# Attention values of three units made together, with three buffers for transposed exponentials and two for decoded words

## The chip, the cores and the metric

The program runs on one core of a Trainium2 chip. The metric is the device time of one execution in microseconds (us). Five engines work side by side, each with its own queue of instructions: TensorE (PE, matrix multiplies; PEld is its weight load), VectorE (DVE), ScalarE (ACT), GpSimd (POOL) and SyncE (SP, which here only issues DMA transfers). They wait for each other on semaphores.

## What is computed

Attention with a local window and a few global columns, then two chains of dense layers, all in float32:

```python
scores = q @ k.T / 8 + bias          # 4 batches, 8 heads, 768 positions, 64 wide
a = softmax(scores where key is one of 8 global or of the last 96 positions)
x = a @ v                            # -> 3072 tokens x 512
x = ((x @ w1) * (x @ w2)) @ w3 @ w_out
h = x @ w_in                         # 512 -> 2048
out = (h * cos(h)) @ w_out2          # 2048 -> 512
```

## The kernel before

**Units and slots.** Attention is cut into 96 units: one unit is 128 query positions of one pair of heads. Twelve units (four head pairs, p, times three position tiles, i) make one block of 384 tokens, and there are eight blocks. After a lead of 14 units, which are made beside the product w3 @ w_out, the main loop runs in slots. Slot n holds the scores of unit n, its maximum, exponential and normalisation, the transposes of unit n - 1, the values of unit n - 2 (the product of the transposed exponentials with v), and one step of the dense layers of an earlier block: in the first eight slots of a block two groups of twelve matmuls of the "up" layers, in the last four two groups of twelve of the "down" layer. The whole order is written out by hand, one queue per engine.

**One slot on each engine.** PE: four score matmuls (lines 544 and 548, into `s_ps`), the values (line 628, into `x_ps`), twelve dense matmuls (lines 391 to 393, into `mm`), the transposes (601, 603, into `pt_ps`), twelve more dense matmuls. DVE: the product of the dense halves (671), the maximum (564), decoding steps, the low half of a dense product (678), the copy of finished values (643), the low half of a coming unit's keys (519, 522), the reciprocal (588), more decoding steps. ACT: the high half of a coming unit (512), of a dense product (675), a decoded word tile (329, 331), the exponential (575), the finished values (642), the dense copy (667), the copy of the transposes to SBUF (611, tile `pt`), another word tile. POOL scales the exponentials (592).

**Values.** `a_values(n)` takes the two tiles `pt` (copied from PSUM in slot n + 1) and `v` (loaded by DMA, line 505) and writes 128 columns of `x_ps`, a PSUM tile of 384 columns which three units of one head pair share; after the third, `a_out` copies it out (642, 643). A matmul of the values fills 64 of PE's columns (form 128*64 or 104*64 in the profile), one per head; every other matmul of the stage fills 128. A unit has 8 matmul records in the trace, or 4 where it lies at the start of a sequence. `pt` and `e` have two buffers, `v` and `qk` three.

**Decoding.** The weights come as 64-bit words. For each of 72 tiles ACT makes `x` and `s` (329, 331), DVE shifts (335), sets signs (339) and adds (347). The last 32 tiles (w_in and w_out2) are then stored to HBM (line 351, `late_w<-x`) for later use. The buffers of `x` are a ring: `x` can be written again only when the store of the tile that had the buffer before has landed. In the first eight slots of the main loop six decoding steps are made in each slot (three steps to a tile), later three in two slots.

**Numbering.** Unit 14 starts at 104 us in the trace, unit 23 at 173 us, and the last values are made at 602 us.

Of the kernel before, what the change touches and what calls it, by code (L numbers as in the profile page):

```python
# [8 lines left out]
F32 = mybir.dt.float32  # L9
# [20 lines left out]
TPB = TB // 128  # L30
# [6 lines left out]
LEAD = 14  # L37
# [225 lines left out]
def fused(ctx, tc, a_qk, a_v, w3p, wo1p, w1p, w2p, winp, wo2p, n_global, n_local, out):  # L263
    nc = tc.nc

    def pool(name, bufs, side="left", space=None):
        kw = {} if space is None else {"space": space}
        if space is None:
            kw["side"] = side
        return tc.alloc_tile_pool(name=name, bufs=bufs, reuse_waits="tile", **kw)  # L270
# [9 lines left out]
    misc = pool("misc", 1)  # L280
    wts = pool("wts", 8)
    attn = pool("attn", 2)
# [19 lines left out]
    rings, taken = {}, {}  # L302
# [50 lines left out]
    def late_load(name, pair):  # L353
        t = raws[name, pair] = misc.tile([128, 2, 512], F32, tag="raw", name="raw", bufs=3)
        src = late_w[0 if name == "in" else 1, 2 * pair:2 * pair + 2]
        nc.sync.dma_start(out=t, in_=src.rearrange("a p b -> p a b"))
# [122 lines left out]
    def where(n):  # L479
        j, r = divmod(n, UPB)  # L480
        p, i = divmod(r, TPB)
        return j, p, i, (TPB * j + i) % (S // 128)

    plain = {}
    qk_raw, v_raw, hh, kl, es, sts, pts, xps, xT = {}, {}, {}, {}, {}, {}, {}, {}, {}

    def a_load(n):
        if not LEAD <= n < NU:
            return
        t = attn.tile([128, QK_W], F32, tag="qk", name="qk", bufs=3)  # L490
        nc.sync.dma_start(out=t, in_=a_qk[n])
        qk_raw[n] = t
# [8 lines left out]
    def a_load_v(n):  # L501
        if not 0 <= n < NU:
            return
        t = attn.tile([128, 2, 128], F32, tag="v", name="v", bufs=3)
        nc.sync.dma_start(out=t.rearrange("p a b -> p (a b)"), in_=a_v[n])
        v_raw[n] = t

    def a_split_hi(n):
        if not LEAD <= n < NU:
            return  # L510
        hh[n] = attn.tile([128, QK_W], F32R, tag="hh", name="hh")
        nc.scalar.copy(out=hh[n], in_=qk_raw[n])  # L512
# [16 lines left out]
    def a_scores(n):  # L529
        if not 0 <= n < NU:  # L530
            return
        s_ps[n] = p_s.tile([128, 2, WIN], F32, tag="s", name="s_ps")
        if n in plain:
            t = plain.pop(n)
            for e in range(2):
                nc.tensor.matmul(
                    s_ps[n][:, e, :], lhsT=t[:, e * 128:(e + 1) * 128],
                    rhs=t[:, 256 + e * WIN:256 + (e + 1) * WIN], start=True, stop=True,
                )
            return  # L540
        t, l = hh.pop(n), kl.pop(n)
        for e in range(2):
            q = t[:, e * 128:(e + 1) * 128]
            nc.tensor.matmul(
                s_ps[n][:, e, :], lhsT=q, rhs=t[:, 256 + e * WIN:256 + (e + 1) * WIN],
                start=True, stop=False,
            )
            nc.tensor.matmul(  # L548
                s_ps[n][:, e, :], lhsT=q, rhs=l[:, e * WIN:(e + 1) * WIN],
                start=False, stop=True,  # L550
            )
# [53 lines left out]
    def a_tcopy(n):  # L605
        if not 0 <= n < NU:
            return
        t = where(n)[3]
        pts[n] = attn.tile([128, 2, 2, 128], F32, tag="pt", name="pt")
        if t:  # L610
            nc.scalar.copy(  # L611
                out=pts[n].rearrange("p a b c -> p (a b c)"),
                in_=pt_ps.rearrange("p a b c -> p (a b c)"),
            )
        else:
            nc.scalar.copy(out=pts[n][:, :, 0, :], in_=pt_ps[:, :, 0, :])

    def a_values(n):
        if not 0 <= n < NU:
            return  # L620
        j, p, i, t = where(n)
        if i == 0:
            xps[j, p] = p_x.tile([128, TB], F32, tag="x", name="x_ps")
        x, pt, vt = xps[j, p], pts.pop(n), v_raw.pop(n)
        for c in range(2 if t else 1):
            kk = NPV if c else 128
            for e in range(2):
                nc.tensor.matmul(  # L628
                    x[e * 64:(e + 1) * 64, i * 128:(i + 1) * 128],
                    lhsT=vt[:kk, c, e * 64:(e + 1) * 64], rhs=pt[:kk, e, c, :],  # L630
                    start=c == 0, stop=c == (1 if t else 0),
                )
# [36 lines left out]
    def up_mult(j, m):  # L669
        ab_f[m] = moe.tile([128, TB], F32, tag="ab_f", name="ab_f", bufs=1)  # L670
        nc.vector.tensor_tensor(out=ab_f[m], in0=mm_ps.pop("b"), in1=a_sb.pop(m), op=ALU.mult)  # L671

    def up_hi(j, m):
        ab[m] = moe.tile([128, 2, TB], F32R, tag="ab", name="ab", bufs=M1)
        nc.scalar.copy(out=ab[m][:, 0, :], in_=ab_f[m])  # L675
# [21 lines left out]
    def down_out(j, m):  # L697
        ps = mm_ps.pop("d")
        t = x2t[j, m] = moe.tile([128, 2, TB], F32R, tag="x2t", name="x2t", bufs=1)
        nc.scalar.copy(out=t[:, 0, :], in_=ps)  # L700
        nc.vector.tensor_tensor(
            out=t[:, 1, :], in0=ps, in1=t[:, 0, :].bitcast(F32), op=ALU.subtract
        )
# [35 lines left out]
    with tc.manual_schedule():  # L739
# [8 lines left out]
        for o in "3A3A3A3A3A3A3A3ABBBBBBBB":  # L748
# [3 lines left out]
            else:  # L752
                n, m = ups.pop(0)
# [7 lines left out]
        tp = pool("tp", 1, side="right")  # L761
        EARLY = 30
        for i, (key, _, _) in enumerate(dec):
            rings[key] = {"raw": [(misc, 3)], "x": [(attn, 3)], "s": [(attn, 2)]}
            if i < EARLY:
                rings[key]["raw"].append((early, 2))
                rings[key]["x"].append((early, 4))
                rings[key]["s"].append((early, 2))
# [51 lines left out]
        def decode(n):  # L820
            for _ in range(n):
                next(steps_left, None)
# [13 lines left out]
        for c, (h, k) in enumerate(chunks):  # L836
            n = c - 2
# [47 lines left out]
        def late(i):  # L885
            if i % 2 == 0:
                return "in", i // 2 + 2
            return ("in", 7) if i == 3 else ("o2", (i - 5) // 2)
# [4 lines left out]
        def x2_load(J, p, tag):  # L893
            t = x2in[J] = p.tile([128, MO, 2, TB2], F32R, tag=tag, name=tag, bufs=1)
            for m in range(MO):
                nc.gpsimd.dma_start(out=t[:, m], in_=x2s[m, :, :, J * TB2:(J + 1) * TB2])

        for j in range(NB1):
            for i in range(UPB):
                sl = j * UPB + i  # L900
                n = sl + LEAD
                last = j == NB1 - 1
                if last and i == 0:
                    attn.release()
                    w2p_ = pool("w2p", 6)
                a_load(n + 4)
                a_load_v(n + 1)
                if last:
                    if i < 3:
                        late_load("in", i)  # L910
                    elif i == 10:
                        late_load("o2", 3)
                    if 2 <= i < 10:
                        late_load(*late(i))
                    if i == 4:
                        x2_load(0, w2p_, "x2in")
                a_scores(n)
                a_values(n - 2)
                a_split_hi(n + 2)
                if 1 <= i <= M1:  # L920
                    up_mult(j, i - 1)
                    up_hi(j, i - 1)
                a_max(n)
                decode(3 if sl < 8 else sl % 2)
                if i == 0 and j > 0:
                    down_out(j - 1, MO - 1)
                    down_store(j - 1, MO - 1)
                elif i > M1:
                    down_out(j, i - M1 - 1)
                    down_store(j, i - M1 - 1)  # L930
                if 1 <= i <= M1:
                    up_lo(j, i - 1)
                a_exp(n)
                a_out(n - 2)
                a_split_lo(n + 2)
                if i < M1:
                    up(j, i, "a")
                    up_copy(j, i)
                else:
                    down(j, i - M1, 0)  # L940
                a_transpose(n - 1)
                a_tcopy(n - 1)
                a_norm(n)
                decode(3 if sl < 8 else 1)
                if i < M1:
                    up(j, i, "b")
                else:
                    down(j, i - M1, 1)
                if last:
                    if i < 3:  # L950
                        run(late_split("in", i, "wC", w2p_))
                    if 2 <= i < 10:
                        run(late_split(*late(i), "wB" if i % 2 else "wA"))
# [75 lines left out]
        for s in range(len(steps) + LAG):  # L1029
# [14 lines left out]
            if s < len(steps):  # L1044
                if J == 0 and m < 5:
                    tag = ("Wa", "Wa", "Wb", "Wb", "wD")[m]
# [85 lines left out]
```

## Time and profile before

| | |
|---|---|
| median of 3 runs | 1190.04 us (1188.34 to 1190.36) |
| the profiled execution | 1191.22 us, its span 1189.4 us |
| lead, 0 to 104.4 us | PE busy 86.9 us |
| main loop, first nine slots, 104.4 to 173.4 | PE busy 57.4 of 69.0 us, DVE 63.1 |
| main loop, the rest, 173.4 to 602.0 | PE busy 428.6 of 428.6 us, DVE 252.1 |
| second chain, 602.0 to 1189.4 | PE busy 578.2 of 587.4 us |

A busy PE is not PE at its peak: matmuls are pipelined and their ends are modelled, so what a step costs is read from the starts of the matmuls that follow each other. The span runs from the first to the last instruction; the time of an execution is some 2 us longer.

### The profile page before, as it was taken

What the parts mean: (1) busy time and instruction counts of PE and PEld (TensorE: products, weight loads), DVE (VectorE), ACT (ScalarE), POOL (GpSimd) and SP (SyncE); (2) the same over time, 40 slices, a digit from 0 to 9 for tenths busy, and PEclk for the clock granted to TensorE, in tenths of its full rate; (3) what the DMA queues carried; (4) which work ended last, traced back from release to release, by engine and by line L of the source; (5) the groups of instructions that cost most, each with busy time, mean ns of one, the idle gap of its engine ahead of it and who ended that gap; (6) DMA issues with size and microseconds to landing.
All of it is one profiled execution on the core that took longest, in us unless ns stands there. A gap on an engine that the chain in (4) does not pass through costs nothing. (4 is left out here: it accounts for less than half of the span.)

```text
span 1189.4 us, 17345 instructions
## 1 busy us (share of the span) xinstructions
PE 1151.1 (97%) x6178; PEld 985.5 (83%) x6178; DVE 769.1 (65%) x1756; ACT 579.6 (49%) x1256; POOL 124.9 (10%) x213
## 2 busy tenths in 40 slices
PE   4998899999999999999999999999999999999997
PEld 1445789999999999999999888888888888888885
DVE  7899986766676555545424666666666666665664
ACT  5777775656566555555434533333333333333332
POOL 0000221111111111111114200000000000000000
PEclk9999999999999999999999999999999999999999
DMA  8776685555554434333145311102102002000001
GB/s 260 251 227 223 232 284 197 176 191 167 168 190 146 132 96 138 90 113 110 45 159 191 125 45 48 59 1 70 38 1 71 36 1 72 36 1 21 16 1 38
DMA packets 65295, 132.72 MB, mean 112 GB/s; under 512 B 6576, under 2 KB 27184, under 8 KB 65200
## 3 DMA queue, kind: packets, MB, share of 16 engines
q1 hardware_dynamic: 58672, 118.95, 30.9%
q0 software_dynamic: 6528, 12.58, 3.7%
q8 instruction: 50, 0.82, 0.3%
q14 instruction: 45, 0.37, 0.1%
HBM read 104.25 MB, written 27.26 MB: 111 GB/s over the span
## 5 line engine op out<-in xcount | busy, mean ns | idle before, releaser
L592 POOL TENSOR_SCALAR e<-e,st 128x232 f32<-128x232 f32 (+1 forms) x164 | 84.5, 528 | 507.3 <-DVE st L588 173.5
L991 ACT ACTIVATE r<-r 128x512 f32<-128x512 f32 x96 | 60.7, 632 | 153.7 <-DVE r L987 153.7
L1000 ACT CAST g<-r 128x512 fp32r<-128x512 f32 x96 | 59.6, 621 | 139.5 <-DVE r L996 139.5
L512 ACT CAST hh<-qk 128x720 fp32r<-128x720 f32 x82 | 65.1, 794 | 118.6 <-PE s_ps L548 111.5
L993 DVE SCALAR_TENSOR_TENSOR r<-r 128x512 f32<-128x512 f32 x96 | 66.5, 693 | 70.0 <-ACT r L991 69.9
L1001 DVE TENSOR_TENSOR g<-r,g 128x512 fp32r<-128x512 f32 x96 | 66.5, 693 | 66.0 <-ACT g L1000 66.0
L575 ACT ACTIVATE e<-e,top 128x232 f32<-128x232 f32 (+1 forms) x192 | 89.3, 467 | 6.9 <-DVE top L564 6.8
L564 DVE CUSTOM_DVE_ANT_0 e<-s_ps,bias 128x232 f32<-128x232 f32 (+1 forms) x192 | 65.5, 378 | 41.8 <-PE s_ps L548 38.8
L391 PE MATMUL mm<-ab,W 128*128 128x384 f32 x256 | 91.8, 358 | 0.5 <-ACT ab L675 0.5
L391 PE MATMUL mm<-xT,wA 128*128 128x384 f32 x256 | 91.7, 358 | 0.0
L391 PE MATMUL mm<-xT,wB 128*128 128x384 f32 x256 | 91.1, 356 | 0.0
L393 PE MATMUL mm<-xT,wA 128*128 128x384 f32 x256 | 86.9, 339 | 0.0
L393 PE MATMUL mm<-ab,W 128*128 128x384 f32 x256 | 86.6, 338 | 0.0
L392 PE MATMUL mm<-xT,wA 128*128 128x384 f32 x256 | 86.4, 338 | 0.0
L392 PE MATMUL mm<-ab,W 128*128 128x384 f32 x256 | 86.3, 337 | 0.1
L393 PE MATMUL mm<-xT,wB 128*128 128x384 f32 x256 | 86.1, 336 | 0.0
L392 PE MATMUL mm<-xT,wB 128*128 128x384 f32 x256 | 85.7, 335 | 0.0
L984 DVE SCALAR_TENSOR_TENSOR r<-kt,h_ps 128x512 f32<-128x512 int32 x96 | 65.7, 684 | 24.3 <-ACT kt L982 24.3
L671 DVE TENSOR_TENSOR ab_f<-mm,a_sb 128x384 f32<-128x384 f32 x64 | 35.5, 555 | 67.5 <-PE mm L393 67.5
L842 PE MATMUL mm<-wo,w 128*128 128x512 f32 x128 | 64.9, 637 | 12.7 <-DVE wo L347 12.7
L982 ACT ACTIVATE kt<-h_ps 128x512 int32<-128x512 f32 x96 | 57.3, 597 | 29.3 <-PE h_ps L393 29.2
L628 PE MATMUL x_ps<-pt,v 128*64 128x128 f32 (+1 forms) x704 | 59.8, 286 | 11.6 <-ACT pt L611 11.4
(189 smaller groups left out, 3017.9 us busy)
## 6 DMA issues: line engine op xcount, KB each, us to landing
qk<-in_a_qk SPq DMA_DIRECT2D x82, 360.0 KB, 3.2
v<-in_a_v SPq DMA_DIRECT2D x97, 128.0 KB, 2.1
x2s<-x2t SPq DMA_DIRECT2D x32, 384.0 KB, 2.9
raw<-in_w3p SPq DMA_DIRECT2D x16, 512.0 KB, 4.7
raw<-in_winp SPq DMA_DIRECT2D x16, 512.0 KB, 4.0
late_w<-x SPq DMA_DIRECT2D x32, 256.0 KB, 2.2
raw<-in_wo2p SPq DMA_DIRECT2D x16, 512.0 KB, 4.1
raw<-late_w SPq DMA_DIRECT2D x16, 512.0 KB, 4.5
```

The costliest lines, as they stand in the source:

```text
L391: nc.tensor.matmul(ps, lhsT=l_hi, rhs=r_hi, start=first and i == 0, stop=False)
L392: nc.tensor.matmul(ps, lhsT=l_hi, rhs=r_lo, start=False, stop=False)
L393: nc.tensor.matmul(ps, lhsT=l_lo, rhs=r_hi, start=False, stop=last and i == n - 1)
L512: nc.scalar.copy(out=hh[n], in_=qk_raw[n])
L564: nc.vector.tensor_tensor_reduce(out=es[n][:, e, :w], in0=sp[:, e, :w], in1=bias[:, 2 * p + e, :], scale=-0.125, scalar=3.0e38, op0=ALU.ad ...
L575: nc.scalar.activation(es[n][:, e, :w], es[n][:, e, :w], ACTF.Exp, bias=top[:, n, e:e + 1], scale=-1.0, accum_out=sts[n][:, 0, e:e + 1],)
L592: (engine or nc.gpsimd).tensor_scalar(es[n][:, e, :w], es[n][:, e, :w], st[:, 1, e:e + 1], 1.0, ALU.mult, ALU.mult)
L842: nc.tensor.matmul(W_ps[m], lhsT=wt["w3", c][:, m * 128:(m + 1) * 128], rhs=wt["wo1", k], start=k == 0, stop=k == M1 - 1,)
L984: nc.vector.scalar_tensor_tensor(out=r, in0=kt, scalar=-C1, in1=ps, op0=ALU.mult, op1=ALU.add)
L991: nc.scalar.activation(r, r, ACTF.Sin, scale=0.5)
L993: nc.vector.scalar_tensor_tensor(out=r, in0=r, scalar=-2.0, in1=r, op0=ALU.mult, op1=ALU.mult)
L1001: nc.vector.tensor_tensor(out=t[:, 1, :], in0=r, in1=t[:, 0, :].bitcast(F32), op=ALU.subtract)
```

## The change

`a_values` is no longer called in every slot for unit n - 2. In every third slot, where n - 2 is the third unit of a head pair, it is called for units n - 4, n - 3 and n - 2, one after the other. So that the transposed exponentials of three units can wait, `pt` gets three buffers (TPB is 3). The ring of decoded words `x` has two buffers in place of three for all tiles from the thirty-first on (six in place of seven for those before). The load of `v` moves: slot n loads unit n - 1, behind the values, where it had loaded unit n + 1 ahead of them; the first main slot loads none and the second loads unit 14 a second time (one load more in all). The number of matmuls is unchanged.

```diff
-        pts[n] = attn.tile([128, 2, 2, 128], F32, tag="pt", name="pt")
+        pts[n] = attn.tile([128, 2, 2, 128], F32, tag="pt", name="pt", bufs=TPB)
...
-            rings[key] = {"raw": [(misc, 3)], "x": [(attn, 3)], "s": [(attn, 2)]}
+            rings[key] = {"raw": [(misc, 3)], "x": [(attn, 2)], "s": [(attn, 2)]}
...
-                a_load_v(n + 1)
...
                 a_scores(n)
-                a_values(n - 2)
+                if (n - 2) % TPB == TPB - 1:
+                    for u in range(n - 1 - TPB, n - 1):
+                        a_values(u)
+                if n > LEAD:
+                    a_load_v(n - 1)
```

On PE, at the scores of unit 45 before (the numbers in the names are buffers; mm and xT belong to the dense layers; x4 are four matmuls of the program, eight records in the trace):

```order
L393 MATMUL mm_3338<-xT_2795,wB_1078 128x384
L544 MATMUL s_ps_3355<-hh_3216 128x232
L548 MATMUL s_ps_3355<-kl_3234,hh_3216 128x232
L544 MATMUL s_ps_3355<-hh_3216 128x232
L548 MATMUL s_ps_3355<-kl_3234,hh_3216 128x232
L628 MATMUL x_ps_3291<-pt_3331,v_3137 64x128 x4
L391 MATMUL mm_3382<-xT_2161,wB_1126 128x384
```

On PE now, at the scores of unit 46, the next third slot:

```order
L393 MATMUL mm_3403<-xT_2793,wB_1158 128x384
L544 MATMUL s_ps_3418<-hh_3289 128x232
L548 MATMUL s_ps_3418<-kl_3302,hh_3289 128x232
L544 MATMUL s_ps_3418<-hh_3289 128x232
L548 MATMUL s_ps_3418<-kl_3302,hh_3289 128x232
L628 MATMUL x_ps_3423<-pt_3254,v_3212 64x128 x4
L628 MATMUL x_ps_3423<-pt_3324,v_3287 64x128 x4
L628 MATMUL x_ps_3423<-pt_3390,v_3351 64x128 x4
L391 MATMUL mm_3457<-ab_2917,W_537 128x384
```

Three units stand in a row between the scores and the dense matmuls; in the two slots between, the dense matmuls follow the scores at once.

On ACT nothing moves, but the waits differ. Before, in the slot of unit 18, where two word tiles are made (the words in brackets are the semaphores, DMAHW those of transfers; of the two DMAHW of line 329, one is the tile's own load and one the store of the tile three earlier):

```order
L329 ACTIVATE x_1304<-raw_1211 128x512 [waits DMAHW6_49,DMAHW5_49]
L331 ACTIVATE s_1306<-raw_1211 128x512 [waits Activation_49]
L575 ACTIVATE e_1295,st_1296<-e_1295,top_85 128x232 [waits DVE_49] x2
L667 COPY a_sb_1328<-mm_1315 128x384 [waits PE_49,Activation_49]
L611 COPY pt_1334<-pt_ps_88 128x512 [waits PE_49]
L329 ACTIVATE x_1345<-raw_1255 128x512 [waits DMAHW7_49,DMAHW0_49]
```

The same place now:

```order
L329 ACTIVATE x_1297<-raw_1209 128x512 [waits DMAHW6_49,DMAHW5_49]
L331 ACTIVATE s_1299<-raw_1209 128x512 [waits Activation_49]
L575 ACTIVATE e_1288,st_1289<-e_1288,top_85 128x232 [waits DVE_49] x2
L667 COPY a_sb_1321<-mm_1308 128x384 [waits PE_49,Activation_49]
L611 COPY pt_1327<-pt_ps_88 128x512 [waits PE_49]
L329 ACTIVATE x_1338<-raw_1253 128x512 [waits DMAHW7_49,DMAHW2_49,DVE_49]
```

The order is the same; the second transfer that line 329 waits for is now the store of the tile two earlier.

## Rows read from the trace of the kernel before

**Rows 1.** Busy time by stretch: PE, PEld, DVE, ACT, POOL, clock, DMA share, GB/s.

```profile
104.40:173.40 69.00, 57.44 (x362) 52.99 (x361) 63.09 (x158) 52.78 (x121) 15.26 (x17) 0.95 0.73 246
173.40:602.00 428.60, 428.60 (x2893) 403.62 (x2892) 252.08 (x784) 244.34 (x622) 69.24 (x148) 1.00 0.44 139
602.00:1189.40 587.40, 578.21 (x2620) 486.18 (x2618) 363.03 (x541) 209.16 (x356) 39.11 (x40) 1.00 0.16 51
```

**Rows 2.** PE's waits, whole span: total us, times, longest.

```profile
PE x_ps L628 <- ACT pt L611: 11.4, 7, 2.5
```

**Rows 3.** Timeline of PE, one slot with 8 value records: start, duration.

```profile
300.57 0.27 PE L544 MATMUL s_ps<-hh 128*128 128x232 f32 x1
...
300.91 0.27 PE L548 MATMUL s_ps<-kl,hh 128*128 128x232 f32 x1
301.11 0.66 PE L628 MATMUL x_ps<-pt,v 128*64 128x128 f32 x8
301.70 0.44 PE L391 MATMUL mm<-xT,wB 128*128 128x384 f32 x1
301.98 0.34 PE L392 MATMUL mm<-xT,wB 128*128 128x384 f32 x1
...
303.73 0.34 PE L393 MATMUL mm<-xT,wB 128*128 128x384 f32 x1
```

**Rows 4.** Timeline of PE, a slot with 4 value records.

```profile
191.09 0.27 PE L548 MATMUL s_ps<-kl,hh 128*128 128x232 f32 x1
191.30 0.44 PE L628 MATMUL x_ps<-pt,v 128*64 128x128 f32 x4
...
191.95 0.34 PE L392 MATMUL mm<-xT,wA 128*128 128x384 f32 x1
```

**Rows 5.** Timeline of PE, from the transposes to the dense matmuls, same slot.

```profile
304.12 0.27 PE L601 MATMUL pt_ps<-ident,e 128*128 128x128 f32 x1
304.23 0.27 PE L603 MATMUL pt_ps<-ident,e 128*104 128x128 f32 x1
304.26 0.42 PE L391 MATMUL mm<-xT,wB 128*128 128x384 f32 x1
304.52 0.33 PE L392 MATMUL mm<-xT,wB 128*128 128x384 f32 x1
```

**Rows 6.** Busy time in that slot, columns as in rows 1.

```profile
300.57:306.45 5.88, 5.88 (x42) 5.55 (x42) 4.01 (x12) 4.26 (x10) 0.90 (x2) 1.00 0.58 165
```

**Rows 7.** Busy time in the decoding slots, columns as in rows 1.

```profile
129.00:168.00 39.00, 32.19 (x218) 29.38 (x217) 36.78 (x92) 30.98 (x72) 10.61 (x12) 1.00 0.82 287
```

**Rows 8.** SP's queue, stores of decoded words: issue time.

```profile
129.51 0.33 SPq L351 DMA_DIRECT2D late_w<-x  x1
...
136.83 0.33 SPq L351 DMA_DIRECT2D late_w<-x  x1
...
157.33 0.33 SPq L351 DMA_DIRECT2D late_w<-x  x1
```

**Rows 9.** Landing of stores: the eleven from 129 to 165 us; those of 136.83 and 157.33.

```profile
DMA to landing us min/median/max: 2.0/3.0/4.8
...
DMA to landing us min/median/max: 4.6/4.6/4.6
...
DMA to landing us min/median/max: 4.8/4.8/4.8
```

**Rows 10.** Timeline of ACT and DVE: a word tile made, and three shifts.

```profile
138.11 0.69 ACT L329 ACTIVATE x<-raw 128x512 f32<-128x512 f32 x1
...
133.85 0.41 DVE L335 TENSOR_SCALAR x<-x 128x512 int32<-128x512 int32 x1
...
140.38 0.41 DVE L335 TENSOR_SCALAR x<-x 128x512 int32<-128x512 int32 x1
...
160.87 0.41 DVE L335 TENSOR_SCALAR x<-x 128x512 int32<-128x512 int32 x1
```

**Rows 11.** The word tiles of line 329 from 173 us on: durations, first and last start.

```profile
L329 ACT ACTIVATE x<-raw x19: 666/671/689, 177.9 to 385.4; 128x512 f32<-128x512 f32 x19
```

## The prediction

> **What bounds the kernel now.** I read the busy time by stretch first [rows 1]. From 173.4 to 602.0 us PE is busy for the whole 428.6 us, with DVE at 252.1 and ACT at 244.3: there the order and the pace of PE's matmuls set the time. In the nine slots before that, 104.4 to 173.4 us, PE is busy for 57.4 of 69.0 us, and PE's waits name the reason: 11.4 us in seven waits of the values for `pt`, ACT's copy of the transposes [rows 2]. That copy is late because DVE is: from 129 to 168 us DVE is busy for 36.8 of 39.0 us and ACT for 31.0 [rows 7], and the small rest is mostly the gaps between DVE's instructions. So the change meets two regimes. Behind 173.4 us it is worth what PE saves; ahead of it, it is worth what DVE saves or loses. The second chain, from 602.0 us on, isn't touched.
>
> **What a visit to the values costs PE.** The timeline of one slot shows it [rows 3]. Three score steps take 300.91 - 300.57 = 0.34 us, or 0.113 each. The last score starts at 300.91; the second dense matmul behind the values starts at 301.98, 1.07 us later. Without values between them this would be one score step and one dense step. A dense step is (303.73 - 301.98) / 10 = 0.175 us (ten steps to the twelfth matmul). So the visit costs 1.07 - 0.113 - 0.175 = 0.78 us. In a slot with four value records in place of eight the same stretch is 191.95 - 191.09 = 0.86 us [rows 4], and the visit costs 0.57. Four records more thus cost 0.21 us, eight cost 0.42, and 0.78 - 0.42 = 0.36 us of the visit don't depend on the number of records. It lies at the edges: 0.20 us from the last score to the first value where a step is 0.113, 0.59 us from there to the first dense matmul where the eight records account for 0.42, and 0.28 us for that dense matmul where a step is 0.175. I use 0.35 us (the rows are rounded to 0.01).
>
> Whether that is an edge of every change of kind, the transposes tell: from their last one at 304.23 to the second dense matmul at 304.52 are 0.29 us, and a transpose step (0.11) with a dense step (0.175) makes 0.285 [rows 5]. Going from transposes back to dense matmuls costs nothing; they fill 128 columns as the dense ones do, the values fill 64. So the cost belongs to going over to the 64-column form and back, and three units in a row pay it once.
>
> **The sum behind 173.4 us.** Slots 23 to 97 make the values of 75 units, 75 visits before and 25 now. 50 visits less at 0.35 us are **17.5 us**. All of it lies on the path, since PE never idles there. The values themselves (0.42 us or 0.21 us a unit) only move: two slots shrink from 5.88 to about 5.1 us, the third grows to about 6.75; together 16.9 in place of 17.6 us. What has to keep up with a slot of 5.1 us is DVE with 4.0 us of work and ACT with 4.3 [rows 6], in slots that a longer one always follows. I cost that at nothing; the cover is about 0.8 us a short slot, and a miss would be paid back in the long one.
>
> The third `pt` buffer and the later `v` load are free here. A load of `v` now stands one slot or more ahead of its use, and only in each third slot does SP wait for the values at that place, as it did in every slot before; the loads of `qk`, the stores and the word loads queued behind it on SP wait no longer than they did. The one load more is not on the path.
>
> **The ring of decoded words.** Here is the price. From the thirty-first tile on `x` has two buffers, so ACT can write a tile only when the store of the tile two earlier has landed; before, three earlier. Behind 173 us a tile is made every (385.4 - 177.9) / 18 = 11.5 us [rows 11], and a store lands in at most 4.8 us [rows 9]: nothing. From 129 to 168 us eleven tiles are made, 3.4 us apart in the mean, and the path is store, landing, ACT's line 329 (0.69 us, and 0.02 until DVE reads it), DVE's shift. What DVE has for it is the time from a store to the shift of the tile two later. The first is 129.51 to 133.85, 4.34 us [rows 8, 10]; the eleven sum to 37.8 us. What is needed is the landing plus 0.71. For the store of 136.83, which landed in 4.6 us, that is 5.31 against 140.38 - 136.83 = 3.55 us: DVE would be 1.8 us late. For that of 157.33 (4.8 us) it is 5.51 against 3.54: 2.0 us late [rows 8 to 10]. The other nine, taken in the same way with their own landings, come to 2.4 us, most of them under 0.6. Together **6.2 us**, on DVE, which has no slack in this stretch.
>
> The bounds: with every landing at the fastest, 2.0 us [rows 9], 2.71 us is enough for all eleven, and the ring costs nothing. With all of ACT's lateness on the path (the eleven tiles would start 15.1 us later in sum than they did) it costs 15.1. I take 6.2, since DVE is the engine without slack and ACT is not. In the lead some tiles now wait for DVE instead of a store; there PE has its own slots to fill, and I cost it at nothing.
>
> In these nine slots the grouping saves nothing: PE waits for `pt` of unit n - 2 at the third slot as it did, and DVE's pace doesn't change. At most six visits of 0.35, 2.1 us, would show.
>
> **Sum.** The profiled execution took 1191.2 us: 1191.2 - 17.5 + 6.2 = 1179.9. It stood 1.2 us above the median of the runs, so I forecast 1178.7 for a median.
>
> **Rivals.** All from the median of 1190.0.
>
> *The ring costs nothing.* Against it stand the landings of 2.0 to 4.8 us; for it, that ACT sometimes waits for DVE anyway. 1190.0 - 17.5 = 1172.5, and 1170.4 with the six visits of the first nine slots.
>
> *ACT's lateness counts whole.* Each late tile also pushes back the exponential and the copies behind it on ACT. 1190.0 - 17.5 + 15.1 = 1187.6.
>
> *Slower: the stores land late throughout.* Place: the eleven tiles from 129 to 168 us. If all landed in 4.8 us, DVE would lose 11 x 5.51 - 37.8 = 22.8 us: 1195.3. It decides from 11 x (L + 0.71) - 37.8 = 17.5, that is L = 4.3 us; the median was 3.0 [rows 9].
> The Trainium skill (DMA: Bandwidth & Descriptors, Latency and other measured facts) gives 0.2 us for an access to HBM on average and 2 us at high load; added to the fastest landing that would be 3.8 us, and as an estimate a loss of 11.8 us, 1184.3. The trace's spread, 2.0 to 4.8 us, is wider than that step.
>
> *The change doesn't do what it says: the cost is paid per unit.* If the 0.35 us came with every unit's first weights, and not with the change of form, three in a row would pay it three times. Then only the ring is left: 1190.0 + 6.2 = 1196.2. Against it: inside a unit, records cost the same 0.05 us each whether there are four or eight, though each pair brings new weights.
> The Trainium skill speaks for either: TensorEngine Tiling (Array Packing), Key Properties, says that changing the tiling mode drains the engine; its Restrictions and Gotchas say that column tiling turns fast weight loads off, which each unit would pay. By the first the sum stays, by the second it is this rival's; the pair of slots in rows 3 and 4 bears out the first.
>
> **Chances.** Forecast 0.68, with its own range 1174 to 1184; ring free 0.12; ACT whole 0.08; paid per unit 0.05; late stores 0.04; a cancelling mix near zero 0.03. About 0.2% (2.4 us) is what a measurement of this kernel can tell from no change. Faster 0.89, the same 0.03, slower 0.08. The range of 1170.5 to 1185.0 holds the forecast and the free ring, and part of the third case.
>
> **What would show it.** In the trace after: 24 value records in a row (20 in some groups) with about 1.5 us from the first to the next dense matmul, where eight now take 0.59; slots of about 5.1, 5.1 and 6.75 us behind the decoding; the values' end about 11 us earlier than 602. Between 129 and 175 us ACT's line 329 should wait for the stores `late_w`, and DVE's shift for line 329, some 6 us in sum. It would be wrong if the third slot took over 7.4 us (paid per unit), if DVE or ACT held PE back in the short slots (a wait of the transposes for POOL, or of the scores for DVE), or if the first nine slots grew by much more than 6 us or not at all.

## The result

The changed kernel takes **1177.35 us** in the median of four runs (1176.75 to 1177.65), the kernel before 1189.82 us in the same comparison (four runs, 1188.34 to 1190.36). The ratio is **0.9896, 95% interval [0.9883, 0.9909]**: 12.5 us faster. The forecast was 1178.7 us, and the range of 1170.5 to 1185.0 us held the time.

Where the time went is read from stretches of the trace, cut at the same places of the program in both kernels: at the first score of unit 14, at the first score of unit 23, and at the last values. The profiled execution of the changed kernel took 1177.65 us, its span is 1175.8 us. Busy time by stretch, columns as in rows 1:

```profile
0.00:105.03 105.03, 86.01 (x308) 42.47 (x309) 90.88 (x274) 73.28 (x159) 1.25 (x9) 0.97 0.77 246
105.03:178.06 73.03, 58.78 (x363) 53.66 (x361) 63.11 (x158) 53.30 (x121) 14.11 (x17) 0.93 0.67 230
178.06:590.04 411.98, 411.98 (x2893) 401.86 (x2892) 254.30 (x786) 244.05 (x622) 72.15 (x148) 1.00 0.46 146
590.04:1175.80 585.76, 577.84 (x2620) 486.17 (x2618) 362.60 (x540) 208.99 (x355) 39.04 (x40) 1.00 0.16 51
```

Against rows 1 three things are to be seen. The stretch behind unit 23 shrank from 428.6 to 411.98 us with the same 2893 matmuls, and PE is busy throughout in both: PE does the same work in less time. The nine decoding slots grew from 69.0 to 73.03 us, though DVE's busy time is the same (63.09 and 63.11 us): DVE waits more there. The lead and the second chain moved by 0.6 and about 1.6 us. With the cuts at two decimals the sum is:

| stretch | before | after | difference |
|---|---|---|---|
| to the first score of unit 14 | 104.41 | 105.03 | +0.6 |
| nine slots, units 14 to 22 | 69.00 | 73.03 | +4.0 |
| from unit 23 to the last value record | 428.40 | 411.80 | -16.6 |
| from there to PE's last matmul | 578.6 | 577.6 | -1.0 |
| what follows | | | -0.6 |
| span | 1189.4 | 1175.8 | -13.6 |

Three slots behind the decoding, of which the third makes the values of three units, and the third's timeline of PE (start, duration); they answer to rows 6 and 3:

```profile
294.74:299.85 5.11, 5.11 (x34) 5.07 (x34) 3.73 (x11) 3.13 (x8) 1.09 (x2) 1.00 0.40 147
299.85:304.90 5.05, 5.05 (x33) 5.02 (x33) 4.09 (x12) 4.23 (x10) 0.99 (x3) 1.00 0.54 167
304.90:311.63 6.73, 6.73 (x57) 6.40 (x57) 4.28 (x12) 3.11 (x8) 1.28 (x3) 1.00 0.42 137
```

```profile
305.23 0.27 PE L548 MATMUL s_ps<-kl,hh 128*128 128x232 f32 x1
305.44 1.54 PE L628 MATMUL x_ps<-pt,v 128*64 128x128 f32 x24
306.91 0.44 PE L391 MATMUL mm<-ab,W 128*128 128x384 f32 x1
307.19 0.34 PE L392 MATMUL mm<-ab,W 128*128 128x384 f32 x1
```

One entry, 0.21 us from the last score to the first value, and one exit, 0.28 us from the first dense matmul to the second, now serve 24 records where they served 8. DVE and ACT are busy for at most 4.2 us of a short slot of 5.05, and PE shows no gap.

The price stands in the waits of the nine slots (total us, times, longest):

```profile
ACT x L329 <- DMA late_w<-x: 8.7, 7, 2.8
...
DVE x L335 <- ACT x L329: 4.7, 5, 2.1
...
PE pt_ps L601 <- POOL e L592: 7.5, 9, 3.2
PE x_ps L628 <- ACT pt L611: 4.1, 2, 2.3
PE mm L391 <- DVE W L851: 2.5, 1, 2.5
```

ACT's line 329 now waits for the stores of decoded words, and DVE's shift for line 329. In the kernel before, the wait of DVE over the same nine slots read:

```profile
DVE x L335 <- ACT x L329: 1.2, 3, 0.6
```

So DVE lost 3.5 us more to this one wait, of the 4.0 us by which the slots grew. PE's own waits changed their names with the grouping: in place of 11.4 us of the values for `pt` [rows 2] there are 7.5 us of the transposes for POOL's exponentials, 4.1 of the values for `pt` and 2.5 of one dense matmul for DVE, 14.1 us in all. In the kernel with the shorter ring alone, below, they are 14.0 us for `pt`.

TensorE's granted clock in these slots was 0.95 of full speed in the mean before and 0.93 now. It doesn't set their length: two of the kernels below take 70.12 us and 73.21 us at 0.93, and two others 68.83 and 68.82 us at 0.98 and 0.95.

### The profile page after: what moved, and what is told of

Its sections match the earlier page's. It is cut to its first block, busy times and chain, and to the rows that moved or that the text cites. A ratio compares the mean times of both kernels' runs of the same rounds, so it can differ in the third digit from the quotient of the medians.

```text
span 1175.8 us, 17351 instructions
## 1 busy us (share of the span) xinstructions
PE 1134.6 (96%) x6178; PEld 984.2 (84%) x6178; DVE 770.9 (66%) x1756; ACT 579.6 (49%) x1256; POOL 126.6 (11%) x213
## 5 line engine op out<-in xcount | busy, mean ns | idle before, releaser
L391 PE MATMUL mm<-xT,wA 128*128 128x384 f32 x256 | 89.5, 350 | 2.5 <-DVE W L851 2.5
L393 PE MATMUL mm<-xT,wA 128*128 128x384 f32 x256 | 86.6, 338 | 0.0
L392 PE MATMUL mm<-xT,wA 128*128 128x384 f32 x256 | 86.2, 337 | 0.0
L990 DVE SCALAR_TENSOR_TENSOR r<-kt,r 128x512 f32<-128x512 int32 x96 | 66.5, 692 | 3.3
```

The source lines that it names most:

```text
L391: nc.tensor.matmul(ps, lhsT=l_hi, rhs=r_hi, start=first and i == 0, stop=False)
L392: nc.tensor.matmul(ps, lhsT=l_hi, rhs=r_lo, start=False, stop=False)
L393: nc.tensor.matmul(ps, lhsT=l_lo, rhs=r_hi, start=False, stop=last and i == n - 1)
L990: nc.vector.scalar_tensor_tensor(out=r, in0=kt, scalar=-C2, in1=r, op0=ALU.mult, op1=ALU.add)
```

## The experiments

The first score of unit 14 stands between 102.4 and 105.1 us in the profiled executions (at 107.3 us in the kernel with the values in the 128-column form), in part because the first scores of all wait for the first transfers and begin between 25.0 and 27.5 us. The experiments are therefore compared by the stretches above as well as by the whole time. The kernel before took 1190.87 us (23 runs) beside the shorter ring alone, the three visits, the sum into the other tile and the grouping from unit 23 on, which ran on one chip, and 1190.66 us (9 runs) beside the other four, on another. Stretches and waits are those of one profiled execution of each kernel.

### The shorter ring alone

The kernel before, with nothing of the change but the ring:

```
-            rings[key] = {"raw": [(misc, 3)], "x": [(attn, 3)], "s": [(attn, 2)]}
+            rings[key] = {"raw": [(misc, 3)], "x": [(attn, 2)], "s": [(attn, 2)]}
```

> The kernel before with the ring of decoded words cut from three buffers to two, and nothing else (values in every slot, two pt buffers). Theory (the ring's wait for a store's landing costs DVE time in the slots of units 14 to 22): those nine slots grow by 4 to 6 us from 69.0, DVE's shift waits some 4 to 5 us for line 329, and the time is 1194 to 1196 us against 1189.8. Rival (the ring is free, and the 4 us that the nine slots grew by come from the grouped values): 1189.8 us, nine slots of 69 us.

Measured: 1194.54 us, ratio 1.0030 [1.0019, 1.0040], 3.6 us slower. The nine slots, and three of their waits:

```profile
104.47:177.68 73.21, 59.03 (x363) 54.18 (x361) 63.20 (x159) 53.43 (x121) 14.09 (x17) 0.93 0.68 232
```

```profile
ACT x L329 <- DMA late_w<-x: 9.6, 8, 2.7
DVE x L335 <- ACT x L329: 4.6, 4, 2.0
PE x_ps L628 <- ACT pt L611: 14.0, 9, 2.4
```

The slots take 73.2 us, as in the changed kernel (73.0), with the waits of ACT and DVE as there (8.7 and 4.7 us); from unit 23 to the last value it takes 428.40 us, as before. The ring alone costs the whole 4 us, nothing outside the nine slots, and the grouping costs and saves nothing inside them. That it has a cost at all takes away the rival of the free ring.

### Three visits in the third slot

The changed kernel, with the three units' values still in the third slot, but each at a place of its own: the second and third between the terms of the dense group behind the scores.

```
             for i, (l, r) in enumerate(terms):
+                if i and i - 1 < len(between):
+                    a_values(between[i - 1])
...
-                if (n - 2) % TPB == TPB - 1:
-                    for u in range(n - 1 - TPB, n - 1):
-                        a_values(u)
+                third = (n - 2) % TPB == TPB - 1
+                if third:
+                    a_values(n - 4)
+                rest = (n - 3, n - 2) if third else ()
```

> The changed kernel, but in each third slot three dense matmuls stand between the values of the first and the second unit and three between the second and the third: the same units in the same slot with 75 visits again behind unit 22. Theory (0.33 us for each change to the 64-column form and back): each third slot takes 0.66 us more, about 7.4 us in place of 6.75, and 25 of them 16.6 us: 1194 us. Rival (a cost per unit or per slot and not per visit, or the gain came from the moved waits): 1177.4 us, third slots of 6.75 us.

Measured: 1193.0 us, ratio 1.0019 [1.0007, 1.0030]. Timeline of PE in the slot that answers to the one above:

```profile
306.14 0.66 PE L630 MATMUL x_ps<-pt,v 128*64 128x128 f32 x8
306.73 0.44 PE L393 MATMUL mm<-ab,W 128*128 128x384 f32 x1
307.01 0.34 PE L394 MATMUL mm<-ab,W 128*128 128x384 f32 x1
307.18 0.33 PE L395 MATMUL mm<-ab,W 128*128 128x384 f32 x1
307.45 0.66 PE L630 MATMUL x_ps<-pt,v 128*64 128x128 f32 x8
308.04 0.44 PE L393 MATMUL mm<-ab,W 128*128 128x384 f32 x1
...
308.75 0.66 PE L630 MATMUL x_ps<-pt,v 128*64 128x128 f32 x8
```

Each return to dense matmuls opens with the same 0.28 us (307.01 - 306.73) and each entry to the values with 0.27 us where a dense step is 0.17. The first score of this slot starts at 305.61 and that of the next at 313.03: 7.42 us, against 6.73 us with the three units in a row. The two visits more cost 0.69 us, 0.35 each. Over 24 such groups, from unit 23's first score to unit 95's, it took 417.51 us against 400.72 in the changed kernel: 16.8 us, and 16.8 / 48 = 0.35 again. The units, their weights and their records are the same in both; only the number of visits differs. The gain is a matter of visits, and the rival that the cost is paid per unit is out.

### Values in the 128-column form

The kernel before, with the same number of value records per slot but all 128 columns of `v` as weights in each, and the loops over heads and halves swapped. Half of what it writes is then the product of one head's exponentials with the other head's values, so the output isn't the attention's.

```
-        for c in range(2 if t else 1):
-            kk = NPV if c else 128
-            for e in range(2):
+        for e in range(2):
+            for c in range(2 if t else 1):
+                kk = NPV if c else 128
...
-                    x[e * 64:(e + 1) * 64, i * 128:(i + 1) * 128],
-                    lhsT=vt[:kk, c, e * 64:(e + 1) * 64], rhs=pt[:kk, e, c, :],
+                    x[:, i * 128:(i + 1) * 128],
+                    lhsT=vt[:kk, c, :], rhs=pt[:kk, e, c, :],
```

> The kernel before with the values made by 128-column matmuls (both heads' v as weights for each head's exponentials; half of each product is meaningless, and the second head's product overwrites the first's, so the output is not attention). Theory (the cost of a visit is the change between the 64-column and the 128-column form): from the last score to the first value one score step, 0.11 us, and the first dense matmul behind the values takes 0.175 us to the next and not 0.28; eight records cost what they cost without edges. Rival (the cost comes with float32 products between others, or with each unit): 0.20 us and 0.28 us stay. No forecast of the total, since each 128-column matmul may take longer than two 64-column ones side by side.

Measured: 1198.93 us, ratio 1.0072 [1.0047, 1.0097], from two runs. Timeline of PE around the values of one slot:

```profile
309.03 0.28 PE L548 MATMUL s_ps<-kl,hh 128*128 128x232 f32 x1
309.15 1.05 PE L628 MATMUL x_ps<-pt,v 128*128 128x128 f32 x8
309.96 0.42 PE L391 MATMUL mm<-ab,W 128*128 128x384 f32 x1
310.22 0.34 PE L392 MATMUL mm<-ab,W 128*128 128x384 f32 x1
```

From the last score to the second dense matmul are 1.19 us. Less a score step and a dense step (0.113 and 0.175, as the prediction took them) 0.90 us are left: eight steps of 0.113, and nothing for an edge. Of the 64-column records 16 more take (306.91 - 305.44) - 0.59 = 0.88 us, 0.055 each in the mean, and a visit with eight costs 0.78, so 0.34 is the edge. The 0.055 isn't the step from one record to the next. The timeline of the changed kernel's group, read up to 305.59, 305.61, 305.70 and 305.72 us, shows that the two heads' records start as a pair and the next pair some 0.11 us behind it, which is what one 128-column record takes:

```profile
305.44 0.33 PE L628 MATMUL x_ps<-pt,v 128*64 128x128 f32 x2
305.44 0.44 PE L628 MATMUL x_ps<-pt,v 128*64 128x128 f32 x4
305.44 0.44 PE L628 MATMUL x_ps<-pt,v 128*64 128x128 f32 x4
305.44 0.55 PE L628 MATMUL x_ps<-pt,v 128*64 128x128 f32 x6
```

The edge therefore belongs to the change between the 128- and the 64-column form. The Trainium skill (TensorEngine Tiling (Array Packing), Key Properties) says that changing the tiling mode drains the engine; the trace agrees, 0.34 us a visit with the change and none without it. The 64-column form is still the better one even at eight records a visit (0.78 against 0.90 us), and the more so at 24. At four it is the worse by as much (0.57 against 4 x 0.113 = 0.45). The whole stretch agrees: of the 75 visits behind unit 23's first score 63 have eight records and 12 have four, 63 x 0.12 - 12 x 0.12 = 6.1 us, and it took 434.46 us where the kernel before took 428.40.

### The sum of the words into the other tile

The changed kernel, with the result of a late word written over `s` and stored from there, so that `x` comes free with DVE's addition and not with a landing:

```
+            nc.vector.tensor_tensor(out=s, in0=x, in1=s, op=ALU.add)
+            xs.pop(key)
+            nc.sync.dma_start(out=late_w[dest[key], key[1]], in_=s.bitcast(F32))
```

> The changed kernel, but the last 32 decoded tiles are summed into the tile s and stored from there, so that x is free again once DVE has read it and only s (line 331, 0.57 us behind line 329 on ACT, not needed by DVE before its sum two steps later) waits for a store. Theory: DVE's shift no longer waits; ACT still does, by up to 0.57 us less a tile; the nine slots go from 73.0 us to about 70, the time to about 1174.5 us (1173 to 1176) against 1177.4. Rival (grouped values cost the 4 us): 1177.4 us.

Measured: 1174.84 us, ratio 0.9867 [0.9847, 0.9887]. The nine slots, and their waits:

```profile
103.00:173.12 70.12, 57.70 (x362) 53.87 (x361) 62.18 (x155) 53.29 (x121) 14.26 (x16) 0.93 0.69 236
```

```profile
ACT s L331 <- DMA late_w<-s: 6.1, 6, 2.5
...
PE x_ps L632 <- DMA v<-in_a_v: 3.1, 1, 3.1
DVE x L335 <- ACT x L329: 3.0, 6, 0.7
```

The wait for the landing now stands before line 331, ACT's writing of `s`, which DVE needs later than `x`; DVE's wait falls from 4.7 to 3.0 us and its longest from 2.1 to 0.7. It was expected to go, and 3.0 us of it stay, where the kernel before had 1.2. The slots take 70.1 us, 2.9 less than in the changed kernel. Of these, 0.9 us is DVE work that lies outside the stretch here (62.18 against 63.11 us busy). The interval of the whole time overlaps that of the changed kernel, so the gain is read from the stretch and is not shown by the ratio. A new row is the 3.1 us for which PE waited for `v`.

### Grouping from unit 23 on only

```
-                if (n - 2) % TPB == TPB - 1:
+                if n < 23:
+                    a_values(n - 2)
+                elif (n - 2) % TPB == TPB - 1:
```

> The changed kernel with the values made in every slot up to the slot of unit 22 and grouped from there on; ring and buffers as in the changed kernel. Theory (in the nine decoding slots DVE sets the pace and grouping neither saves nor costs): 1177.4 us within 1.5, nine slots of 73 us with PE waiting for pt again in place of POOL. Rival (long third slots cost the 4 us there): 1173.4 us, nine slots of 69 us.

Measured: 1175.33 us, ratio 0.9863 [0.9845, 0.9881], 0.6 us below the lower end of what was expected; behind unit 23 411.75 us, as with grouping throughout. The nine slots took 73.47 us, but not for one reason alone:

```profile
PE x_ps L628 <- DMA v<-in_a_v: 6.8, 3, 3.8
PE x_ps L628 <- ACT pt L611: 6.7, 3, 2.5
```

PE waited 6.8 us for `v`, which in this kernel is loaded one slot ahead of its use, its issue standing between stores on SP's queue. What the slots would take without that wait isn't to be had from this run, so it doesn't bear on the ring. That grouping in the nine slots is worth nothing rests on the ring alone against the changed kernel.

### The changed kernel again

> The changed kernel once more, beside the three others of this set. Expected: 12 to 13 us faster than the kernel before, nine slots of units 14 to 22 at 73 us.

Measured: 1176.65 us, ratio 0.9883 [0.9867, 0.9899], 14.0 us faster than the kernel before and a little more than expected; nine slots 73.4 us, 411.75 us from unit 23 to the last value. PE waited once for `v` in the nine slots:

```profile
PE x_ps L628 <- DMA v<-in_a_v: 3.1, 1, 3.1
```

In the profiled execution of the first comparison that row is missing. The load was issued at 142.86 us in both; it landed after 4.9 us there and after 6.1 us here. Of the 3.1 us most is no loss: at the same place PE waited 2.3 us for `pt` in the first execution, and here the copy of `pt` ended at 147.70 us and the values started at 149.13. So the later load of `v`, which the prediction called free, can land some 1.4 us behind `pt`. What that costs isn't shown: the nine slots were 0.4 us longer, and DVE's waits for line 329 were longer too (5.7 in place of 4.7 us).

### The loads of v moved behind the group

The kernel of the sum into `s`, and the three loads of `v` for the next group right behind the group that frees their buffers:

```
-                if n > LEAD:
-                    a_load_v(n - 1)
+                    for u in range(n - 1, n - 1 + TPB):
+                        a_load_v(u)
```

> The kernel that sums late words into s, and the v tiles of the next three units loaded together behind each group of values (no load in the two slots between, none twice). Theory: what is left of the nine slots' growth in the run that sums into s (70.1 against 69.0 us, with one wait of 3.1 us of PE for a v tile) goes; nine slots 68 to 69.5 us, the time 1.0 us under that run, about 17 us under the kernel before. Rival (the wait for v lay beside DVE's work): nine slots 70 us, the same time as that run.

Measured: 1172.02 us, ratio 0.9854 [0.9838, 0.9870]. The nine slots, and their waits:

```profile
102.59:171.42 68.83, 55.60 (x362) 50.59 (x361) 61.99 (x155) 53.01 (x121) 14.54 (x16) 0.98 0.71 237
```

```profile
PE pt_ps L605 <- POOL e L596: 8.2, 10, 3.2
...
DVE x L335 <- ACT x L329: 2.2, 4, 0.9
```

No wait of PE for `v` is left, and the slots are at 68.8 us, as they were before the change (69.0) and as expected; the whole time fell by 2.8 us against the sum into `s`, on another chip, where 1.0 was expected. The 16.6 us behind them are untouched: 411.79 us. Against the changed kernel the slots gained 4.2 us: DVE's wait for line 329 fell from 4.7 to 2.2 us, 1.1 us is DVE work that lies outside the stretch (61.99 against 63.11 us), and the rest was not separated.

### The lead grouped too

The kernel of the last experiment, with the values of the lead's units in threes as well:

```
-                a_load_v(n + 1)
+                if n in (-1, 0):
+                    a_load_v(n + 2)
...
-            a_values(n - 2)
+            if n >= 2 and (n - 2) % TPB == TPB - 1:
+                for u in range(n - 1 - TPB, n - 1):
+                    a_values(u)
+                for u in range(n - 1, n - 1 + TPB):
+                    a_load_v(u)
```

> As the one before, and the values grouped in the lead as well (units 0 to 11 in four groups in place of twelve visits). In the lead scores and dense matmuls differ in form too (64*128 and 128*128), so that a visit there adds 0.33 us less the 0.20 us that going from scores to dense matmuls costs anyway: 8 x 0.13 = 1 us at most, if DVE (busy 41.3 of 44.0 us there) lets PE have it. Expected 0 to 1 us faster than the run before it.

Measured: 1171.33 us, ratio 0.9844 [0.9826, 0.9862], with unit 14 at 102.89 us and the nine slots at 68.82 us, against 102.59 and 68.83 in the kernel it was made from. The nine slots here:

```profile
102.89:171.71 68.82, 57.10 (x363) 52.26 (x362) 61.98 (x155) 53.31 (x121) 14.26 (x16) 0.95 0.72 240
```

The two can't be told apart, and whether the visits saved in the lead are worth the expected 0 to 1 us stays open: the granted clock from 27 to 102 us was 0.96 here and 0.98 in the kernel it was made from, and 0.02 of 75 us is 1.5 us, more than the gain looked for. The runs of the two overlap (1171.59 to 1174.32 us and 1170.16 to 1173.77). Both kernels are faster than the changed one on the same chip by some 5 us (1172.02 and 1171.33 against 1176.65; none of their ten runs is as slow as the fastest of its four), and they are the fastest of this study.

A ring of three word tiles together with the grouping wasn't tried; the third `pt` is of the size of the word tile given up for it (512 float32 a partition each).

## Why the prediction held

**The cost of a visit: right, a little too large.** The prediction took 0.35 us and 50 visits, 17.5 us. The stretch from unit 23 to the last value shrank by 428.40 - 411.80 = 16.6 us, 0.33 a visit; measured over the 24 full groups it is (416.64 - 400.72) / 48 = 0.332, and 0.35 where two visits a group were put back. The cause that it argued from two slots of four and eight records, a change of form and not a cost of the units, is shown: inserted visits cost it again, and values in the 128-column form don't pay it. One detail of the argument doesn't hold: not every other matmul fills 128 columns. Those of line 603 fill 104 (128*104 in rows 5), and they pay no edge either; what pays it here is the 64-column form. The slots came out at 5.11, 5.05 and 6.73 us against the forecast 5.1, 5.1 and 6.75, and the group at 306.91 - 305.44 = 1.47 us against 1.5.

**The short slots: right.** That DVE and ACT keep up in 5.1 us was costed at nothing; PE is busy for all of it.

**The ring: right in kind, too large.** The path, store, landing, ACT's line 329, DVE's shift, is the one in the waits, and the ring alone costs the slots 4.2 us, the changed kernel 4.0, where 6.2 was forecast. The term that was mis-sized is the lateness summed over eleven tiles with the landings of the kernel before, and it was wrong in two ways. First, it added up the lateness of tiles that follow each other. While DVE waits for one tile, the store of the tile between has already been issued, so that this store gets the wait as time to land. Below, the store of 141.47 stands before DVE's late shift of 143.56 and has until the next, 146.44, that is 4.97 us where it had 2.96 before (140.48 to 143.44); it landed in 3.2 us, and DVE didn't wait. The prediction's own sum, with each wait taken off the lateness of the next tile, is 4.9 us in place of 6.2. Second, the landings were others. In the changed kernel the eleven stores from 128 to 172 us landed so:

```profile
DMA to landing us min/median/max: 2.1/2.3/5.2
```

The spread is about that of rows 9, but the median is 2.3 us in place of 3.0. With these landings the sum taken in this way gives 4.0 us, with those of the shorter ring alone 4.2, and with those of the changed kernel's second profiled execution 5.0, where the slots grew by 4.4. These are estimates from the landings of each trace and the spacing of stores and shifts in the kernel before. DVE waited for line 329 five times, 4.7 us in sum, of which the kernel before had 1.2 already. Which tile pays is a matter of which store meets a late landing. The kernel with three visits, with the same ring, took 71.0 us for the nine slots, with 61.3 us of DVE's work inside them in place of 63.1; so a price of about 4 us is good to a microsecond or so. The worst store, in the timeline of SP, ACT and DVE (in brackets the idle time before and what ended it):

```profile
137.57 0.33 SPq L351 DMA_DIRECT2D late_w<-x  x1
141.47 0.33 SPq L351 DMA_DIRECT2D late_w<-x  x1
142.87 0.66 ACT L329 ACTIVATE x<-raw 128x512 f32<-128x512 f32 x1 [2.84 <-DMA late_w<-x]
143.56 0.43 DVE L335 TENSOR_SCALAR x<-x 128x512 int32<-128x512 int32 x1 [2.12 <-ACT x L329]
146.44 0.42 DVE L335 TENSOR_SCALAR x<-x 128x512 int32<-128x512 int32 x1
```

The store of 137.57 took 5.2 us to land; ACT stood for 2.84 us and DVE, 0.69 us behind it, for 2.12. A landing so late was in the price; that all were so late, the rival on the slower side with its 4.3 us, did not come. That rival's price has the same double counting: eleven landings of 4.8 us cost 13.2 us when each wait is taken off the next, not 22.8, and the change would still have gained.

**ACT's lateness whole: no.** ACT waited 8.7 us for the stores, and the slots grew by 4.0. What ACT loses counts as far as DVE has to wait for it.

**The nine slots' grouping: nothing, as forecast.** The ring alone makes them as long as the ring and the grouping together.

**The later load of v: not always free.** The prediction put it at nothing, and some executions show PE waiting for it once, 3.1 us, of which 1.4 go beyond the wait for `pt` in the changed kernel's second execution. It argued from the distance of a load from its use in slots. The load was issued one slot ahead as it said; but with a landing of 4.9 us it was just in time and with one of 6.1 us it was late.

**The rest.** The lead grew by 0.6 us, within what it varies by; the stretch from the last values to the last matmul, costed at nothing, shrank by 1.0 us, of which 0.5 is one wait of PE for ACT that the changed kernel doesn't show, and the tail by 0.6, where it varies between 8.3 and 9.1 us in the executions. What did the rest was not tested. The two terms' errors partly offset: 0.9 us too much gained by the visits against 2.2 too much lost to the ring, and 1.0 from the rest. So the forecast's total came closer than its ring did, in part by luck. Its chances have a slip: the cases that it prices as slower add up to 0.09, not 0.08.

## What to carry to other kernels

Where PE is busy without a gap, look at the steps between starts of matmuls and not at durations: a step that is longer where two forms of matmul meet is a cost per visit, and putting the visits together takes it off without taking any work away. Pay for the buffer that this needs where a wait for a transfer doesn't reach the engine that sets the pace: here the words summed into the tile that DVE needs later, and the loads of `v` moved to the point where their buffers come free, together gave back what the shorter ring had cost. When waits for transfers follow each other closely, don't add them up one by one: a wait gives the next transfer as much more time. And check an edit in the regime where it acts: the same grouping was worth 0.33 us a visit where PE set the pace and nothing where PE was waiting.

## What the runs showed of the hardware

The change from 128- to 64-column weights and back costs PE 0.33 to 0.35 us, and nothing where the form stays, nor between dense matmuls and transposes of 128 and 104 columns. A record of 128 columns takes 0.11 us, and so does a pair of 64 columns each, one for either half, which start together. The landing of one and the same kind of store, in the same stretch, varied from 2.1 to 5.2 us with the DMA engines busy for 0.67 of the time; a sum of landings is better bounded by its spread than taken from one execution. And one load, issued at the same time in two executions of the same kernel, landed after 4.9 us in one and after 6.1 in the other.
